# W' products by quarters of the model width on four column groups, block transposes on VectorE, and one-hot bursts kept apart

## The chip, the core and the metric

The kernel runs on one core of a Trainium2 chip. A core has TensorE (PE, matmuls into the eight banks of PSUM), VectorE (DVE), ScalarE (ACT), GpSimd (POOL) and SyncE (SP, which only issues transfers here). The metric is the time of one execution on the device in microseconds; the time of a kernel is the median of its runs.

## The reference

Tokens `x` are 2,048 rows of 640. The output mixes two branches with a gate per token, `g = sigmoid(sum(x * gate_w))`:

```
a = x @ dft_hid_re.T ;  b = x @ dft_hid_im.T
y = dft_seq_re @ a - dft_seq_im @ b              # branch A: 2048 x 2048 by 2048 x 640, twice

q = x @ w_q                                      # branch B: 32 heads of 2 x 128
s1 = q1 @ k1.T ; s2 = q2 @ k2.T                  # 16 keys in each half: 64 x 16 scores per token
top 2 of s1, top 2 of s2, top 2 of their 4 sums -> experts e of 256, weights softmax
act = gelu(x @ u[e]) ; out = sum(weight * act * v[e])

result = g * y + (1 - g) * out
```

## The kernel before

**Arithmetic.** A product in single precision is made of three matmuls on rounded parts (`mm3`, lines 137 to 141): high by high, high by low, low by high. `split` (line 132) makes the parts: ACT copies the high part, DVE or POOL subtracts it from the value. Matmuls on unrounded f32 data are also used, in one place that the change touches.

**W'.** The scores need `x @ (w_q @ k)`. So the kernel does not form q: it first multiplies `w_q` with the keys to a matrix W' of 640 x 1,024 (64 half heads by 16 keys), kept as high and low parts in `WU[0]` and `WU[1]`, with the rows (d, in five blocks of 128) on the partitions. The products have the keys as weights (`kp`, 128 x 32: two halves r of a pair side by side, one of them zero, so that two products add up in the same 32 rows of PSUM) and `w_q` as the data that streams through. As a key product has only 32 columns of weights, four of them stand side by side on the four column groups of the array, and write the rows 32j to 32j+31 of one PSUM bank.

In the kernel before, a group G takes eight half heads; column group j holds one pair of them, and the 640 columns of d are streamed in two halves of 320 (`w_part`, line 522; four loads of `wq` a group, 32 in all, through five buffers `wq`). Two calls of `w_part` make a burst. ACT copies the two banks to `wp` (line 535). The result has the keys on the partitions, and W' needs d there: `w_transposes` (line 537) turns it by TensorE, five blocks of 128x128 with the identity `identf`, into bank 7, four blocks at one place and one at the next; ACT copies the high part to WU (line 543), DVE subtracts (line 544).

**Order of the first stage.** Branch A's sums over the sequence run all the time. They are cut in pieces: `seq_piece(n)` multiplies one 128 x 512 block of a DFT matrix (loaded to `wf`, split to the ring `WS`) with x, 5 blocks of d by 3 matmuls, into banks 0 to 4; 16 pieces are a chunk, at whose end ACT copies the five banks to `ST` (line 303). A step n is a piece and what was hung behind it by `at(n, f)`; `follow(n)` emits those in the order in which they were hung. Steps 0 to 12 also load and split x (`load_x`, `split_x`), `gate_sum` sums the gate on DVE, and `gate` (line 598) at step 14 makes the sigmoid on ACT and stores the 2,048 values to `gdr` on ACT's queue. The bursts hang behind steps 4, 6, 8, 10, 12, 14, 16, 17, 18, 19, 20, 22, 23, 24, 25 and 27 with the transposes of the group before them; the stage ends with step 30 (`N0` is 31), and the scores begin. All loads are issued by SP in program order, so a load that waits for its buffer holds back the loads behind it.

**The background.** From then on the selection of the top scores and the experts run on DVE beside the matmuls of branch A. They are generators in a `Pump`: after each `mm3`, `run_bg` adds its time (0.68 us) to a clock `bg.now` and, times a share, to a credit, and takes as many steps of the generators as the credit pays for; a step yields its cost, or -1.0 where it cannot go on yet. `experts` (line 862) turns the chosen experts into one-hot rows and columns on DVE (`build`, three operations for two groups of tokens, into one of eight sets `mid`), and `use` (line 900) multiplies them on TensorE: a burst of 64 matmuls of 32 columns on the four column groups, into bank 7, which ACT copies to `cd` (line 889) and, after every second burst, stores to `gd` with two transfers (line 895). There are 16 such bursts. They are emitted with two groups of built sets behind (`behind(2)`), or all at once when the sets run out (`behind(0)`), and `bg.drain` at step NPC-18 takes whatever is left. `NPC` is 152, the number of pieces; the last quarter of branch A's sums, 16 pieces, begins at NPC-16.

Of the kernel before, what the change touches and what calls it, by code (L numbers as in the profile page):

```python
# [8 lines left out]
F32 = mybir.dt.float32  # L9
# [3 lines left out]
OP = mybir.AluOpType  # L13
# [3 lines left out]
P = 128  # L17
# [11 lines left out]
KD = D // P  # L29
HALF = D // 2  # L30
NG = HH // 8
NB = 4
GSCALE = 32768.0
FAR = -3.0e38
# [66 lines left out]
def gated_mix_kernel(ctx: ExitStack, tc: tile.TileContext, xT, xn, dreT, dimT, wsre, wsim, wq, kT, uT, vv, gw, out):  # L101
# [17 lines left out]
    def ps_s(shape=(P, TC)):  # L119
        return bank(5 + rotate("pss", 2), shape)  # L120

    def ps_t(shape, dt=F32):
        return bank(7, shape, dt)
# [94 lines left out]
    def at(n, f, *args):  # L218
        then.setdefault(n, []).append(lambda: f(*args))
# [272 lines left out]
    gate_sum(1)  # L492
    io = p1.tile([P, P], F32)
    identf = const.tile([P, P], F32)
    wtab4 = const.tile([P, E, 4], F16)
# [4 lines left out]

    def fill_ident():
        nc.gpsimd.iota(io, pattern=[[1, P]], base=0, channel_multiplier=-1, allow_small_or_imprecise_dtypes=True)
        nc.gpsimd.tensor_scalar(identf, io, 0.0, None, op0=OP.is_equal)

    def fill_rest():
        nc.gpsimd.iota(wtab4, pattern=[[-1, E], [0, 4]], base=E, channel_multiplier=0,
                       allow_small_or_imprecise_dtypes=True)

    at(1, fill_kp)
    at(4, fill_ident)  # L510
    at(6, fill_rest)

    wqs, wps, wp = {}, {}, {}
    WQB = 5
    NWQ = 4 * NG

    def load_wq(m):
        if m < NWQ:
            wqs[m] = p1.tile([P, 4, HALF], F32, name="wq", bufs=WQB)
            nc.sync.dma_start(wqs[m], wq[m])  # L520

    def w_part(m):
        G, r, n = m // 4, m // 2 % 2, m % 2
        if r == 0:
            wps[G, n] = ps_s()
        ps = wps[G, n]
        w = wqs.pop(m)
        for j in range(4):
            nc.tensor.matmul(ps[32 * j:32 * j + 32, :HALF], kp[:, 8 * G // H, r, :], w[:, j], start=(r == 0),  # L529
                             stop=(r == 1))  # L530
        load_wq(m + WQB)
        if r == 1:
            if n == 0:
                wp[G] = p1.tile([P, D], F32, name="wp", bufs=1)
            nc.scalar.activation(wp[G][:, n * HALF:(n + 1) * HALF], wps.pop((G, n))[:, :HALF], AF.Copy)  # L535

    def w_transposes(G, k0, k1):
        f = wp[G]
        t = ps_t([P, 4, P])
        for k in range(k0, k1):  # L540
            nc.tensor.transpose(t[:, k - k0, :], f[:, k * P:(k + 1) * P], identf)  # L541
        h, l = (WU[G // 4][:, n, k0:k1, P * (G % 4):P * (G % 4 + 1)] for n in range(2))
        nc.scalar.activation(h, t[:, :k1 - k0], AF.Copy)  # L543
        nc.vector.tensor_sub(l, t[:, :k1 - k0], h.bitcast(F32))  # L544

# [29 lines left out]
    for n in range(NT - 2):  # L575
        at(n, gate_sum, n + 2)
    for m in range(WQB):
        at(m, load_wq, m)

    bursts = [4 + m if m < 14 else 17 + (m - 14) * 10 // 16 for m in range(0, NWQ, 2)]  # L580
    n = bursts[-1]
    bursts += [n + 1, n + 2]
    for j, b in enumerate(bursts):
        if j >= 2:
            at(b, w_transposes, j // 2 - 1, *((4, KD) if j % 2 else (0, 4)))
        if 2 * j < NWQ:
            at(b, w_part, 2 * j)
            at(b, w_part, 2 * j + 1)
    n += 3
    at(n - 8, load_xT, 0)  # L590
# [271 lines left out]
    def experts():  # L862


        cd = {}

# [32 lines left out]

        def use(group):  # L900
            shape = (P, 16, E * 2)
            t = bank(7, shape)
            for a, (g, c, s) in enumerate(group):
                pt, qt = (HOT[s // 2][:, n, s % 2].rearrange("p (m c j) -> p m c j", m=16, j=2) for n in range(2))
                for m in range(16):
                    for j in range(2):
                        r = slice(64 * (m % 2) + 32 * j, 64 * (m % 2) + 32 * j + 32)
                        nc.tensor.matmul(t[r, 8 * a + m // 2, :], pt[:, m, :, j], qt[:, m, :, j], start=True,  # L908
                                         stop=True)
                free_sets.append(s)  # L910
            bg.now += 0.9 * len(group)
            bg.credit += 0.9 * len(group)
            whole = len(group) == 2 and group[0][1] % 2 == 0
            for a, (g, c, s) in enumerate(group[:1] if whole else group):
                sums(g, c, t if whole else t[:, 8 * a:8 * a + 8])
                yield 0.2
# [7 lines left out]
        while todo:  # L924
            if len(free_sets) < min(2, len(todo)):
                yield from behind(0)
            while todo[0][0] and len(rowed) < NT:
                yield -1.0
            k = min(len(todo), 2)
            group = [(*todo.popleft(), free_sets.popleft()) for n in range(k)]  # L930
            (g, c, s), odd = group[0], group[-1][2] % 2
            assert k == 1 or s % 2 == 0 and odd
            yield from build(g, c, s, k, 1.2 if k == 2 else 0.75)
            built.append(group)
            yield from behind(2)
# [263 lines left out]
    for n in range(N0, NPC):  # L1199
# [21 lines left out]
        if n == NPC - 28:  # L1221
            mid_wf.clear()
            for t in [t for t in wf_tags if t[0] is None]:
                wf_tags.remove(t)
        if n == NPC - 18:
            bg.drain()
# [56 lines left out]
```

## Time and profile before

| | |
|---|---|
| median of 3 runs | 766.51 us (764.39, 766.51, 767.0) |
| the profiled execution | 764.58 us, span 762.7 us |
| granted clock of TensorE | 1.00 |
| bytes moved | 162.00 MB, mean 212 GB/s |
| loads of `wq` | 32 of 640 KB, 6.9 us from issue to landing (median) |

The span is what the profile shows from the first instruction to the last; the time of the execution has about 2 us more around it. The chain of work that ended last is followed back from the last instruction; its rows give start, duration, engine and line. A row of the timeline gives start, duration, engine, line, operation, tiles, shapes and count, and in brackets how long the engine stood idle before and for what. A row of the windows gives the stretch, its length, the busy time of PE, PEld, DVE, ACT and POOL with the count of instructions, the granted clock, the share of the DMA engines and GB/s. PE rows overlap, since matmuls are pipelined: one of 512 columns is busy for 0.39 us, and the next starts 0.23 us after it.

### The profile page before, as it was taken

To read this page: it belongs to the slowest core of one execution; us is meant where nothing else is said; L and a number is where in the kernel's file an instruction comes from. 1 tells how busy PE (TensorE), PEld (TensorE's weight loads), DVE (VectorE), ACT (ScalarE), POOL (GpSimd) and SP (SyncE) were. 2 spreads that over 40 slices of the span, in tenths; PEclk is the share of its full clock that TensorE was granted. 3 is DMA by queue.
4 is the path that set the end of the run, shared out by engine and by line. 5 is a ranking of instruction groups with operands and counts; after the bars stand their busy time and mean duration, and the time that the engine had idled before them with its cause. 6 is when DMAs were issued, how large, how long until landed. Compare 5 with 4: busy or idle time off the path is not lost.

```text
span 762.7 us, 12203 instructions
## 1 busy us (share of the span) xinstructions
PE 754.8 (99%) x4568; PEld 611.1 (80%) x4568; DVE 584.7 (77%) x667; ACT 303.5 (40%) x500; POOL 371.8 (49%) x283
## 2 busy tenths in 40 slices
PE   9999999999999999999999999999899999999997
PEld 6777667888888888888888888787788888888886
DVE  7742031377989999999999999999779999648661
ACT  5334224322323452435232464444345553543441
POOL 4523224456756494757475501642013484587253
PEclk9999999999999999999999999999999999999999
DMA  9976985636455657372944868799754785776302
GB/s 337 390 263 195 292 338 218 204 120 215 138 189 159 196 195 256 106 232 94 319 149 144 267 202 254 213 359 283 206 190 141 261 301 169 226 255 196 125 28 70
DMA packets 109629, 162.00 MB, mean 212 GB/s; under 512 B 34497, under 2 KB 49985, under 8 KB 109569
## 3 DMA queue, kind: packets, MB, share of 16 engines
q1 hardware_dynamic: 78960, 133.02, 52.8%
q10 hardware_dynamic: 26960, 15.87, 7.0%
q0 software_dynamic: 3648, 12.32, 4.7%
q8 instruction: 36, 0.59, 0.3%
q14 instruction: 25, 0.20, 0.1%
HBM read 122.90 MB, written 36.71 MB: 209 GB/s over the span
## 4 chain that ended last, share of the span: by engine, by line
PE 98%; ACT 1%; DMA 0%; ACTq 0%; issue 0%; DVE 0%; DVEq 0%
PE b L139 32%; PE b L141 31%; PE b L140 31%; PE b L529 2%; PE b L908 1%; PE b L541 1%; PE b L293 0%; DMA xr<-in_xn 0%; ACT WS L134 0%; ACT ST L303 0%; ACT L599 0%; ACT cd L889 0%; ACTq L895 0%; ACT wp L535 0%; DVE ST L1173 0%
## 5 line engine op out<-in xcount | busy, mean ns | idle before, releaser
L139 PE MATMUL b<-WS,X 128*128 128x512 f32 x520 | 205.6, 395 | 0.4 <-ACT ST L303 0.3
L140 PE MATMUL b<-WS,X 128*128 128x512 f32 x520 | 202.8, 390 | 0.0
L141 PE MATMUL b<-WS,X 128*128 128x512 f32 x520 | 202.6, 390 | 0.0
L135 POOL TENSOR_TENSOR WS<-wf,WS 128x512 fp32r<-128x512 f32 x76 | 111.5, 1473 | 154.9 <-ACT WS L134 139.3
L139 PEld LDWEIGHTS b<-WS,X 128*128 128x128 f32 x520 | 97.6, 188 | 29.7 <-issue 7.8
L134 ACT ACTIVATE WS<-wf 128x512 fp32r<-128x512 f32 x116 | 72.7, 629 | 117.6 <-PE b L141 43.7
L141 PEld LDWEIGHTS b<-WS,X 128*128 128x128 f32 x520 | 97.6, 188 | 20.8
L140 PEld LDWEIGHTS b<-WS,X 128*128 128x128 f32 x520 | 97.7, 188 | 19.4 <-DVE WS L135 0.2
L635 ACT ACTIVATE sc<-b 128x512 f32<-128x512 f32 x32 | 19.5, 608 | 118.5 <-PE b L141 109.0
L135 POOL TENSOR_TENSOR WS<-ra,WS 128x512 fp32r<-128x512 f32 x40 | 59.1, 1495 | 11.8 <-ACT WS L134 11.5
L141 PE MATMUL b<-WU,xl 128*128 128x512 f32 x160 | 62.2, 389 | 0.0
L139 PE MATMUL b<-WU,xh 128*128 128x512 f32 x160 | 62.2, 389 | 0.0
L140 PE MATMUL b<-WU,xh 128*128 128x512 f32 x160 | 62.2, 389 | 0.0
L135 POOL TENSOR_TENSOR WP<-ra,WP 128x512 fp32r<-128x512 f32 x20 | 32.4, 1635 | 47.8 <-ACT WP L134 47.8
L650 DVE TENSOR_TENSOR ew<-sc,mm 128x1024 f16<-128x1024 f32 x32 | 54.4, 1700 | 1.1
L134 ACT ACTIVATE WS<-ra 128x512 fp32r<-128x512 f32 x56 | 35.1, 631 | 49.7 <-PE b L141 31.2
L1028 DVE TENSOR_TENSOR ra<-ra 128x512 f32<-128x512 f32 x48 | 49.9, 1086 | 2.9 <-POOL WP L135 2.7
L544 DVE TENSOR_TENSOR WU<-b,WU 128x512 fp32r<-128x512 f32 (+1 forms) x16 | 7.8, 490 | 57.5 <-ACT WU L543 57.5
L648 DVE TENSOR_REDUCE mm<-sc 128x64 f32<-128x1024 f32 x32 | 38.9, 1215 | 16.4 <-ACT sc L635 15.9
L314 POOL DMA_DIRECT2D tq<-td x32 | 17.6, 552 | 56.2 <-PE b L141 56.2
L654 DVE TENSOR_REDUCE rr<-ew 128x64 f16<-128x1024 f16 x32 | 39.0, 1220 | 1.1
L652 DVE TENSOR_TENSOR ew<-ew 128x1024 f16<-128x1024 f16 x32 | 37.4, 1168 | 1.1
(190 smaller groups left out, 1547.7 us busy)
## 6 DMA issues: line engine op xcount, KB each, us to landing
wq<-in_wq SPq DMA_DIRECT2D x32, 640.0 KB, 6.9
ra<-pd SPq DMA_DIRECT2D x70, 256.0 KB, 3.9
wf<-in_wsre SPq DMA_DIRECT2D x63, 256.0 KB, 4.7
wf<-in_wsim SPq DMA_DIRECT2D x46, 256.0 KB, 3.9
sa<-in_wsim SPq DMA_DIRECT2D x32, 256.0 KB, 3.0
sd<-sa SPq DMA_DIRECT2D x32, 256.0 KB, 3.2
tq<-td POOLq DMA_DIRECT2D x32, 256.0 KB, 5.1
xf<-in_xT SPq DMA_DIRECT2D x8, 640.0 KB, 5.4
```

The lines of the kernel that those rows point to most:

```text
L134: nc.scalar.activation(h, f, AF.Copy)
L135: eng.tensor_sub(l, f, h.bitcast(F32))
L139: nc.tensor.matmul(o, wh, ah, start=first, stop=False, skip_group_check=more)
L140: nc.tensor.matmul(o, wh, al, start=False, stop=False, skip_group_check=more)
L141: nc.tensor.matmul(o, wl, ah, start=False, stop=last, skip_group_check=more)
L314: nc.gpsimd.dma_start(t.bitcast(F32), td[k, :, ("s1", "s3", "a22", "s2").index(what)])
L635: nc.scalar.activation(scs[i].rearrange("p h e -> p (h e)")[:, c], ps, AF.Copy)
L648: nc.vector.tensor_reduce(m, sc, op=OP.max, axis=AX.X)
L650: nc.vector.tensor_tensor(eq, sc, m[:, :, None].to_broadcast([P, HH, E]), op=OP.is_equal)
L652: nc.vector.tensor_tensor(eq, eq, wtab, op=OP.mult)
L654: nc.vector.tensor_reduce(r, eq, op=OP.max, axis=AX.X)
L1028: nc.vector.tensor_add(take((b, o, k)) if f is not None else raw[b, o, k], raw[b, o, k] if f is None else f, raw[b, what, k])
```

## The change

1. **W' by quarters of d.** A column group no longer holds a pair of heads but a quarter of d, and a head pair's 640 columns become 160 on each group (5 blocks k of 32). Three head pairs are streamed together, 480 columns, in a burst of 8 matmuls into one bank: 11 bursts (`W_BURSTS`), ten of three pairs and one of two. The sixth crosses from the first half of the pairs to the second, which has other keys, and is made in two parts of 160 and 320 columns. They hang behind steps 6, 9, 12, 14, 16, 18, 20, 22, 24, 26 and 28.
2. **Block transposes.** As the four quarters lie on the four strips of 32 partitions, only 32x32 blocks have to be turned: `wq_out`, one step behind the burst, has one DVE transpose of 128x480 from PSUM to `wr`, from which ACT writes the high part to WU and DVE subtracts the low. The transposes on TensorE, the copies to `wp` and the identity go.
3. **Loads.** `wq` lies in memory by partition now, 163,840 bytes each, burst after burst. A burst is four loads of 480 KB (128 x 960 values; the last burst 2 x 320 each), and there are two buffers of four loads. The loads of bursts 0 and 1 hang one behind each of the steps 0 to 7; those of burst b+2 stand behind burst b, two at its step and two at the next.
4. **One-hot bursts.** `use` waits until `bg.now` is 3.0 us past the last burst; a burst adds 0.85 a group to the credit and nothing to `bg.now`; when the sets run out, one group is used and not all; the drain moves from NPC-18 to NPC-15.

```diff
+W_BURSTS = [range(n, min(n + 3, H)) for n in range(0, H, 3)]
...
-    for j in range(4):
-        nc.tensor.matmul(ps[32 * j:32 * j + 32, :HALF], kp[:, 8 * G // H, r, :], w[:, j], start=(r == 0),
-                         stop=(r == 1))
-    load_wq(m + WQB)
-    if r == 1:
-        if n == 0:
-            wp[G] = p1.tile([P, D], F32, name="wp", bufs=1)
-        nc.scalar.activation(wp[G][:, n * HALF:(n + 1) * HALF], wps.pop((G, n))[:, :HALF], AF.Copy)
...
-    for k in range(k0, k1):
-        nc.tensor.transpose(t[:, k - k0, :], f[:, k * P:(k + 1) * P], identf)
...
+    def load_wq(b, *parts):
+        if b < len(W_BURSTS):
+            c, n = W_BURSTS[b][0] * 2 * D, len(W_BURSTS[b])
+            if b not in wqs:
+                wqs[b] = p1.tile([P, 2, 4, 3 * KD * 32], F32, name="wq", bufs=2)
+            for i in parts:
+                nc.sync.dma_start(wqs[b][:, i // 2, i % 2 * 2:i % 2 * 2 + 2, :n * KD * 32],
+                                  wq[:, c:c + n * 2 * D].rearrange("p (i j x) -> p i j x", i=4, j=2)[:, i])
+
+    def w_burst(b):
...
+        for half, lo, hi in ((0, 0, k), (1, k, len(ms))):
...
+            c = slice(lo * KD * 32, hi * KD * 32)
+            for r in range(2):
+                for j in range(4):
+                    nc.tensor.matmul(ps[32 * j:32 * j + 32, c], kp[:, half, r, :], w[:, r, j, c], start=(r == 0),
+                                     stop=(r == 1))
+
+    def wq_out(b):
+        ms = W_BURSTS[b]
+        f = p1.tile([P, 3, KD, 32], F32, name="wr", bufs=1)
+        nc.vector.transpose(f[:, :len(ms)].rearrange("p i k e -> p (i k e)"), wps.pop(b)[:, :len(ms) * KD * 32])
...
+            nc.scalar.activation(h, t, AF.Copy)
+            nc.vector.tensor_sub(l, t, h.bitcast(F32))
...
+    for i in range(8):
+        at(i, load_wq, i // 4, i % 4)
+    for b, n in enumerate((6, 9, 12, 14, 16, 18, 20, 22, 24, 26, 28)):
+        at(n, w_burst, b)
+        at(n, load_wq, b + 2, 0, 1)
+        at(n + 1, wq_out, b)
+        at(n + 1, load_wq, b + 2, 2, 3)
...
         def use(group):
+            while bg.now < last[0] + 3.0:
+                yield -1.0
...
-            bg.now += 0.9 * len(group)
-            bg.credit += 0.9 * len(group)
+            last[0] = bg.now
+            bg.credit += 0.85 * len(group)
...
-                yield from behind(0)
+                yield from behind(len(built) - 1)
...
-        if n == NPC - 18:
+        if n == NPC - 15:
             bg.drain()
```

On PE, behind piece 14 (`b` is a bank of PSUM, `WS` and `X` the parts of the DFT block and of x), before:

```order
L140 MATMUL b_150<-WS,X 128x512
L141 MATMUL b_150<-WS,X 128x512
L541 MATMUL b_612<-identf,wp 128x128
L529 MATMUL b_559<-wq,kp 32x320 x4
L529 MATMUL b_566<-wq,kp 32x320 x4
L139 MATMUL b_146<-WS,X 128x512
```

and in the changed kernel, at the same place (its lines are numbered one to six lower):

```order
L139 MATMUL b_148<-WS,X 128x512
L140 MATMUL b_148<-WS,X 128x512
L528 MATMUL b_572<-wq,kp 32x480 x8
L138 MATMUL b_144<-WS,X 128x512
L139 MATMUL b_144<-WS,X 128x512
```

The transpose is gone, and eight matmuls of 320 columns into two banks are eight of 480 into one; behind pieces 4, 8, 10, 17, 19, 23, 25 and 27 no burst stands any more, and behind 9, 26 and 28 stands one that was not there.

On ACT, around the end of the first chunk (`zc` is the gate, `gdr` its store, `ST` the copies of the five banks), before:

```order
L543 ACTIVATE WU<-b_612 128x128
L535 ACTIVATE wp<-b_559 128x320
L535 ACTIVATE wp<-b_566 128x320
L599 ACT_TABLE_LOAD
L599 ACTIVATE zc<-zc 128x16
L600 DMA gdr<-zc 128x16x1
L134 ACTIVATE WS<-wf 128x512
L303 ACTIVATE ST<-b_146 128x512
```

and in the changed kernel:

```order
L542 ACTIVATE WU<-wr 128x5x96
L133 ACTIVATE WS<-wf 128x512
L593 ACT_TABLE_LOAD
L593 ACTIVATE zc<-zc 128x16
L594 DMA gdr<-zc 128x16x1
L133 ACTIVATE WS<-wf 128x512
L302 ACTIVATE ST<-b_144 128x512
```

The copies of the burst behind piece 14 stood ahead of the gate; now the write of the burst behind piece 12 does, with a split between them, and that of the burst behind piece 14 comes after the five copies to `ST`.

On ACT, at the last one-hot bursts (`cd` is the copy of bank 7, `gd` its stores, `ring` and `mid` further places of the split blocks), before:

```order
L889 ACTIVATE cd<-b_5144 128x32x16
L134 ACTIVATE WS<-wf 128x512 x2
L889 ACTIVATE cd<-b_5239 128x32x16
L895 DMA gd<-cd 1024x1x32 x2
L889 ACTIVATE cd<-b_5307 128x32x16
L889 ACTIVATE cd<-b_5374 128x32x16
L895 DMA gd<-cd 1024x1x32 x2
L134 ACTIVATE WS<-mid 128x512
```

and in the changed kernel:

```order
L883 ACTIVATE cd<-b_5136 128x32x16
L889 DMA gd<-cd 1024x1x32 x2
L133 ACTIVATE ring<-mid 128x512
L133 ACTIVATE ring<-wf 128x512
L883 ACTIVATE cd<-b_5223 128x32x16
L324 ACTIVATE ST<-b_3515 128x512
L324 ACTIVATE ST<-b_3516 128x512
L133 ACTIVATE WS<-wf 128x512
L883 ACTIVATE cd<-b_5311 128x32x16
L889 DMA gd<-cd 1024x1x32 x2
```

The last three copies stood together; splits and the copies of other banks stand between them now. On PE, 15 ordinary matmuls or more lie between any two bursts.

More of the change, by code (lines that the diff above doesn't have):

```diff
@@ L29 @@
 KD = D // P
-HALF = D // 2
-NG = HH // 8
 NB = 4
+W_BURSTS = [range(n, min(n + 3, H)) for n in range(0, H, 3)]
 GSCALE = 32768.0
@@ L492, in gated_mix_kernel @@
     gate_sum(1)
-    io = p1.tile([P, P], F32)
-    identf = const.tile([P, P], F32)
     wtab4 = const.tile([P, E, 4], F16)
@@ L499, in fill_kp @@
             nc.gpsimd.tensor_copy(kp[:, :, r, r * E:(r + 1) * E], kt)
-    def fill_ident():
-        nc.gpsimd.iota(io, pattern=[[1, P]], base=0, channel_multiplier=-1, allow_small_or_imprecise_dtypes=True)
-        nc.gpsimd.tensor_scalar(identf, io, 0.0, None, op0=OP.is_equal)
     def fill_rest():
@@ L509, in gated_mix_kernel @@
     at(1, fill_kp)
-    at(4, fill_ident)
     at(6, fill_rest)
[L513 to L527, printed above, removed]
-        for j in range(4):
-            nc.tensor.matmul(ps[32 * j:32 * j + 32, :HALF], kp[:, 8 * G // H, r, :], w[:, j], start=(r == 0),
-                             stop=(r == 1))
-        load_wq(m + WQB)
-        if r == 1:
-            if n == 0:
-                wp[G] = p1.tile([P, D], F32, name="wp", bufs=1)
-            nc.scalar.activation(wp[G][:, n * HALF:(n + 1) * HALF], wps.pop((G, n))[:, :HALF], AF.Copy)
@@ L537, in w_transposes @@
-    def w_transposes(G, k0, k1):
-        f = wp[G]
-        t = ps_t([P, 4, P])
-        for k in range(k0, k1):
[L541 to L544, printed above, removed]
+    wqs, wps = {}, {}
+    NWH = H // 2
+    def load_wq(b, *parts):
[6 more added lines that the diff above has]
+                                  wq[:, c:c + n * 2 * D].rearrange("p (i j x) -> p i j x", i=4, j=2)[:, i])
@@ new lines, in w_burst @@
+    def w_burst(b):
+        ms = W_BURSTS[b]
+        wps[b] = ps = ps_s((P, TC))
+        w = wqs.pop(b)
+        k = sum(m < NWH for m in ms)
+        for half, lo, hi in ((0, 0, k), (1, k, len(ms))):
+            if lo == hi:
+                continue
+            c = slice(lo * KD * 32, hi * KD * 32)
[3 more added lines that the diff above has]
+                                     stop=(r == 1))
@@ new lines, in wq_out @@
+    def wq_out(b):
+        ms = W_BURSTS[b]
+        f = p1.tile([P, 3, KD, 32], F32, name="wr", bufs=1)
+        nc.vector.transpose(f[:, :len(ms)].rearrange("p i k e -> p (i k e)"), wps.pop(b)[:, :len(ms) * KD * 32])
+        for i, m in enumerate(ms):
+            if i and m % NWH:
+                continue
+            n = min(len(ms) - i, NWH - m % NWH)
+            t = f[:, i:i + n].rearrange("p i k e -> p k i e")
+            h, l = (WU[m // NWH][:, a, :, 32 * (m % NWH):32 * (m % NWH + n)].rearrange("p k (i e) -> p k i e", i=n)
+                    for a in range(2))
+            nc.scalar.activation(h, t, AF.Copy)
+            nc.vector.tensor_sub(l, t, h.bitcast(F32))
@@ L576, in gated_mix_kernel @@
         at(n, gate_sum, n + 2)
[L577 to L589, printed above, removed]
+    for i in range(8):
[5 more added lines that the diff above has]
+        at(n + 1, load_wq, b + 2, 2, 3)
+    n = 30
     at(n - 8, load_xT, 0)
@@ L862, in experts @@
     def experts():
-        cd = {}
+        cd, last = {}, [0.0]
         def build(g, c, s, n, us):
@@ L1260 @@
     x = ins["A_x"][0]
+    wq = ins["B_w_q"].reshape(KD, 4, 32, H // 2, 2, 2, P).transpose(6, 5, 3, 4, 1, 0, 2).reshape(P, H, 2, 4, KD * 32)
     arrays = {
@@ L1267 @@
         "wsim": seq(ins["A_dft_seq_im"]),
-        "wq": rows(ins["B_w_q"].reshape(2, HALF, H // 8, 4, 2, 2, P).transpose(5, 2, 4, 0, 6, 3, 1)
-                   .reshape(4 * NG, P, 4, HALF)),
+        "wq": rows(np.concatenate([wq[:, b[0]:b[-1] + 1].transpose(0, 2, 3, 1, 4).reshape(P, len(b) * 2 * D)
+                                   for b in W_BURSTS], axis=1)),
         "kT": rows(np.stack([ins["B_k1"].T, ins["B_k2"].T], axis=1)),
```

## The prediction

> **What bounds the kernel now.** I read the busy table of the page first, then the chain that ended last, then the windows of the two stretches that the change touches.
>
> ```profile
> PE 754.8 (99%) x4568; PEld 611.1 (80%) x4568; DVE 584.7 (77%) x667; ACT 303.5 (40%) x500; POOL 371.8 (49%) x283
> by line: PE b L139 31.6%; PE b L141 30.7%; PE b L140 30.7%; PE b L529 2.5%; PE b L908 1.2%; PE b L541 0.6%; PE b L293 0.5%; DMA xr<-in_xn 0.4%; ACT WS L134 0.2%; ACT ST L303 0.2%; ACT L599 0.2%; ACT cd L889 0.2%; ACTq L895 0.2%; issue 0.1%;
> 20.00:138.00 118.00, 117.75 (x693) 84.36 (x692) 37.70 (x60) 41.56 (x82) 42.03 (x33) 1.00 0.80 281
> 466.00:549.00 83.00, 80.92 (x1325) 64.42 (x1324) 79.29 (x90) 36.56 (x62) 28.81 (x32) 1.00 0.87 264
> ```
>
> TensorE is busy for 99% of the span and carries nearly the whole chain. So a microsecond of matmul stream that is taken away is a microsecond of the end, as long as nothing else becomes late. The window rows give span, then PE, PEld, DVE, ACT, POOL busy time, the granted clock, the DMA share and GB/s. In the first stretch (20 to 138 us, the W' products) DVE works 37.7 of 118 us and ACT 41.6, so both have room. In the second (466 to 549 us, the one-hot bursts) DVE works 79.3 of 83 us. The clock is 1.00 in both, so no term below is scaled.
>
> **Term 1, the W' products.** Three places of the chain show what they cost today: a burst alone, one behind a single transpose, one behind four.
>
> ```profile
> 21.84 0.23 PE b L141
> 22.07 1.22 PE b L529 x16
> 23.28 0.43 PE b L139
> 23.71 0.24 PE b L140
> ...
> 47.32 0.11 PE b L541
> 47.43 1.21 PE b L529 x16
> 48.65 0.43 PE b L139
> ...
> 38.63 0.44 PE b L541 x4
> 39.08 1.21 PE b L529 x16
> 40.29 0.43 PE b L139
> ```
>
> An ordinary matmul takes 0.23 us of the chain. A burst takes 1.22, and the matmul behind it 0.43, so 0.20 more, and the next four 0.01 more each: 1.46 us. With one transpose it is 0.11 + 1.21 + 0.20 + 0.04 = 1.56, with four 0.44 + 1.21 + 0.20 + 0.03 = 1.88. The program has 16 bursts: two alone, seven of each other kind; a last group of four transposes and a last single one stand alone (0.5 and 0.1). Together 2 x 1.46 + 7 x 1.56 + 7 x 1.88 + 0.6 = 27.6 us. The shares by line agree: L529 and L541 have 3.1% of 762.7, 23.7 us, and 16 x 0.24 behind the bursts makes 27.5.
>
> The new bursts do the same number of column steps, 32 x 160 columns on four groups, in 11 pieces and not 16, and no transposes. What a wider burst costs is seen inside an old one, in narrow slices of the timeline:
>
> ```profile
> 22.00 0.48 PE L529 MATMUL b<-wq,kp 128*32 128x320 f32 x4
> 22.56 0.45 PE L529 MATMUL b<-wq,kp 128*32 128x320 f32 x4
> 22.83 0.45 PE L529 MATMUL b<-wq,kp 128*32 128x320 f32 x4
> ```
>
> Four matmuls, one on each column group, start together, and the next four start 0.27 us later (22.83 - 22.56): a burst is four such rounds of 320 columns. At 480 columns a round takes 0.27 x 1.5 = 0.405, so a burst grows by 4 x 0.135 = 0.54 to 2.00 us. Were the whole burst to scale, it would be 2.2; were the start of a round to cost something of its own, below 2.00. I take 2.00, since start and end of a burst (1.46 - 1.08 = 0.38) do not depend on its width. Nine full bursts make 18.0, the sixth, which crosses from one half of the heads to the other in eight shorter rounds, 2.05 with a little for the seam, the last, of 320 columns, 1.46. Sum 21.5 us, **saving 6.1** (4.3 if all of a burst scales).
>
> What the transposes become: 11 block transposes of 128x480 on DVE, 12 copies on ACT and 12 subtractions on DVE, for 16 + 16 copies on ACT and 16 subtractions on DVE.
>
> ```profile
> L544 DVE TENSOR_TENSOR WU<-b,WU 128x512 fp32r<-128x512 f32 (+1 forms) x16 | 7.8, 490 | 57.5 <-ACT WU L543 57.5
> L458 DVE CUSTOM_DVE_ANT_0 xr<-xr,gwb 128x640 f32<-128x640 f32 x12 | 15.8, 1312 | 0.0
> 20.56 0.82 DVE L135 TENSOR_TENSOR X<-xr,X 128x640 fp32r<-128x640 f32 x1
> 26.79 0.39 PE L139 MATMUL b<-WS,X 128*128 128x512 f32 x1
> ```
>
> No block transpose is in this trace. By the nearest rows it takes between 0.49 us (a subtraction of the same data) and 1.3 us (the slowest operation of the stretch); I take 0.7. The Vector Engine (DVE) Microarchitecture Reference of the Trainium skill (3.8, reshape front-end) says that it sustains one element per cycle and lane, which at the 0.96 GHz of the skill's main page (NeuronCore Architecture) would be about 0.5 us, an estimate; the sum would be the same. For at either end, 11 x 1.3 + 12 x 0.7 = 23 us come in for 7.8, on an engine that idles 80 us of this stretch. The transpose waits for a burst that ended a whole step (15 matmuls, 3.4 us) before; queued behind it on DVE are the low halves of x, and these are early: the one that ends at 21.38 feeds the step that starts at 26.79, and without the first burst that step starts 1.5 us sooner. WU is first read two steps after the last write. So DVE and ACT cost nothing here; without that cover, each late write would show as one wait of under 1.5 us.
>
> **Term 2, the wait at the end of step 15.**
>
> ```profile
> 65.69 0.77 ACT L535 ACTIVATE wp<-b 128x320 f32<-128x320 f32 x2 [0.83 <-PE b L529]
> 66.47 1.28 ACT L599 ACT_TABLE_LOAD   x1
> ...
> 68.01 0.39 ACTq L600 DMA_DIRECT2D gdr<-zc  x1
> ...
> 69.03 0.39 PE L141 MATMUL b<-WS,X 128*128 128x512 f32 x1
> 69.04 2.53 ACT L303 ACTIVATE ST<-b 128x512 f32<-128x512 f32 x5
> 69.67 0.50 PE L139 MATMUL b<-WS,X 128*128 128x512 f32 x1 [0.25 <-ACT ST L303]
> ```
>
> ACT waits for the burst (L535), then loads the sigmoid's table, and so comes late to copy the five full banks; PE starts its next chunk 0.64 us after the last matmul, not 0.23, and a start after a gap costs another 0.11 (0.50 for 0.39). The changed order has no copy of W' ahead of the table load: ACT is there as soon as step 13 has freed a slot, at about 4.7 + 14 x 3.4 + 3 x 2.0 = 58.5, and issues the store of the gate at about 60.8, not 68.0. **Saving 0.5** (between 0, if another wait takes the place, and 0.5).
>
> **Term 3, what that earlier store meets.** Behind it the transfers nearly stop:
>
> ```profile
> 70.00:75.00 5.00, 5.00 (x36) 3.40 (x34) 0.53 (x1) 3.20 (x7) 1.78 (x2) 1.00 0.76 151
> 75.00:80.00 5.00, 5.00 (x37) 3.34 (x33) 0.46 (x2) 0.71 (x2) 1.30 (x1) 1.00 0.60 33
> 80.00:85.00 5.00, 5.00 (x35) 3.58 (x35) 0.26 (x1) 1.55 (x3) 1.29 (x1) 1.00 0.79 248
> 85.00:100.00 15.00, 15.00 (x94) 10.65 (x88) 1.41 (x3) 4.28 (x8) 3.88 (x3) 1.00 1.02 401
> ```
>
> From about 72 to 82 us 33 to 151 GB/s move, and 401 after it. The store writes 2,048 single words; that it is the cause is inferred from its place. Before, five buffers of 640 KB lie ahead of PE, and PE has no gap there. The new program has two buffers of 1.97 MB (four loads of 480 KB), and the load of burst b+2 waits on SP for the end of burst b. With the store 7 us sooner the slow stretch falls at about 65 to 75 us. Burst 5, counted from 0, is loaded from the end of burst 3, about 4.7 + 15 x 3.4 + 4 x 2.0 = 63.7, into the middle of it. Its 1.97 MB and one piece of 0.26 then need 5.6 us at 401 GB/s, to 80.6, or a microsecond less with what trickles through (33 GB/s for 10 us). PE wants them at 4.7 + 19 x 3.4 + 5 x 2.0 = 79.3. A wait of 0.3 to 1.3 us, or none if the slow stretch is shorter: I take **0.5 lost**. On SP the loads of the pieces stand behind the waiting loads, but they go out five steps ahead of PE.
>
> **Term 4, the one-hot bursts.**
>
> ```profile
> 467.32 0.60 PE b L908 x63
> 467.92 0.43 PE b L139
> ...
> 544.23 0.66 PE b L908 x61
> 544.91 0.61 ACT cd L889
> 545.54 0.52 ACTq L895
> 546.10 0.69 ACTq L895
> 546.91 0.61 ACT cd L889
> 547.56 0.66 PE b L908 x64
> 548.22 0.43 PE b L139
> ```
>
> A burst alone costs 0.60 + 0.20 + 0.03 = 0.83 us; 13 of them, two 0.1 longer, make 11.0. The last three stand back to back, and since all use bank 7, each waits until ACT has copied the one before and issued its stores: 544.23 to 548.22 and the slow restart, 4.22 us. In the new order the closest two have 15 ordinary matmuls between them, 3.4 us; ACT needs 0.61 for the copy and 1.21 for two stores. So 16 x 0.83 = 13.3 for 15.2: **saving 1.8** (1.6 if the two long ones stay long and more follow; 0 if the waits only move). DVE builds the same one-hots, some one or two pieces later, up to a burst in the second piece of the last quarter. The bound is that DVE, busy 79.3 of 83 us, then holds up a split that PE waits for; up to the 1.8 gained.
>
> **Sum.** 6.1 + 0.5 - 0.5 + 1.8 = 7.9 us. The profiled execution took 764.58 (span 762.7 and 1.9 around it): 756.7. Its time is 1.9 below the median of the three runs, which would give 758.6. The four known executions lie in two pairs, 764.4 and 764.6, 766.5 and 767.0; I forecast from their middle, 765.5, and say **757.6 us**. A measurement of this kernel can tell about 0.3% (2.3 us) from no change, so faster means below 764.2.
>
> **Rivals.**
> - *W' comes late more than once.* From the end of burst 2 (55) to the start of the last (123.5) the new program moves 13.1 MB of W', 17 pieces of 0.26, and 2.6 of stores and small loads: 20.3 MB in 68 us, less 9 lost to the store, or 342 GB/s against the 401 seen. For: with two buffers nothing is in store, and a late burst delays the next load. Against: the margin of 15%. At 320 GB/s it costs 4 us: about 761.5.
> - *Slower: the new layout of W' loads badly.* Rows were 5,120 bytes of one block; now each partition reads 3,840 bytes from its own row of 163,840. This trace has no such pitch. If it brings the rate below 20.3 / (59.4 + 7.9) = 302 GB/s, three quarters of 401, the gain is gone; at 280 the stretch is 13 us longer, some 771 us. Against it: the whole slack of 15% goes first. A rule of the Trainium skill speaks for this rival: DMA: Bandwidth & Descriptors (Latency and other measured facts) has row pitches at large powers of two slow down, 512 KiB to 207 GB/s of 214, 4 MiB to 103. By its figures 160 KiB would lose at most 3%, an estimate, and this rival would not come; no run here shows it.
> - *The spacing only moves the waits* (DVE or ACT late at the same place): 1.8 less, 759.4. For it speaks DVE's 96%; against it that PE idles only 83.00 - 80.92 = 2.1 us in that stretch, and the chain puts them between the last three bursts, behind ACT.
> - *A burst scales as a whole* (2.2, not 2.00), so the fewer bursts save only 4.3: also 759.4. The rows of the rounds speak against it.
>
> **Chances.** Forecast (no or one short wait) 0.62; W' late by 2 to 6 us 0.18; spacing without effect 0.10; bursts that scale 0.04; slower by the layout 0.06. The range takes the low pair of executions with the full gain (6.1 + 0.5 + 1.8 = 8.4, and 0.5 should rounds grow by less than their width: 755.5, rounded to 755.0) and reaches up to 762.5, W' late by 5. Faster 0.62 + 0.10 + 0.04 + most of 0.18 = 0.91, same 0.04, slower 0.05.
>
> **What would show it.** Chain: 11 bursts of 2.0 us, no transposes, 21.5 us in all; step 15 to 16 without the 0.64. Windows: 33 GB/s some 7 us earlier, then perhaps one idle of PE ahead of the sixth burst that ends with a DMA of wq. One-hot bursts all alone at 0.6. I am wrong if PE has waits for wq at several bursts, if a round of 480 takes over 0.41, or if DVE's block transposes take over 2 us.

## The result and the profile after

| | before | changed |
|---|---|---|
| median (range) of six runs | 765.88 us (764.39 to 767.0) | 758.03 us (756.76 to 759.05) |
| ratio of the two, 95% interval | | 0.9899 (0.9881 to 0.9918) |
| profiled execution (span) | 764.58 us (762.7) | 759.05 us (757.3) |

The medians differ by 7.85 us. The two profiled executions differ by 5.5: that of before is near the fastest of its six, that of the changed kernel is the slowest of its six. What follows explains the 5.4 us between the two spans; 0.1 lies around them.

The busy table of the page, its chain by line, and the windows of the two stretches of the changed kernel (W' products 20 to 132 us, one-hot bursts 461 to 552 us):

```profile
PE 750.0 (99%) x4464; PEld 604.9 (80%) x4464; DVE 591.9 (78%) x674; ACT 296.5 (39%) x480; POOL 376.4 (50%) x281
PE b L138 30%; PE b L139 29%; PE b L140 29%; PE b L528 2%; DMA wq<-in_wq 2%; DMA mid<-in_wsim 1%; PE b L904 1%; DVE WS L134 1%; DMA mid<-sd 1%; PE b L292 1%; DMA gd<-cd 0%; PE b L480 0%; DVE mid L875 0%; ACTq L889 0%; SPq L191 0%
20.00:132.00 112.00, 111.26 (x587) 77.99 (x586) 48.38 (x67) 35.99 (x62) 40.27 (x31) 1.00 0.86 290
461.00:552.00 91.00, 89.65 (x1359) 70.32 (x1358) 82.49 (x96) 38.71 (x68) 31.13 (x31) 1.00 0.83 251
```

TensorE is still busy for 99%, at clock 1.00. What is new in the chain are transfers: `wq` with 2%, `mid` with another 2%. The chain of the kernel before has less than 1% of transfers.

**The W' bursts.** The chain at a full burst, and at the sixth:

```profile
41.30 1.75 PE b L528 x16
43.05 0.43 PE b L138
43.48 0.24 PE b L139
...
68.14 0.60 SPq L514
...
68.79 12.71 DMA wq<-in_wq
...
81.55 1.54 PE b L528 x18
83.09 0.43 PE b L138
```

A full burst is 1.75 in the chain and 0.20 in the matmul behind it. Counted over the starts of all matmuls it costs 2.00 us, nine times alike, and the last 1.47. The sixth waits: a load of `wq` that SP issued at 68.14 needs 12.71 us. The timeline of PE has the burst's first part beginning at 79.89, and the rest only at 81.55:

```profile
79.57 0.39 PE L140 MATMUL b<-WS,X 128*128 128x512 f32 x1
79.89 0.93 PE L528 MATMUL b<-wq,kp 128*32 128x160 f32 x12
81.55 1.28 PE L528 MATMUL b<-wq,kp 128*32 128x160 f32 x18 [0.74 <-DMA wq<-in_wq]
```

From 79.89 to the next ordinary matmul at 83.09 are 3.20 us; without a wait this burst takes 1.76 (first row of e3 below). So the wait costs 1.4 us with its slow restart. Why the load is so slow is in the windows of 5 us (the last number of a row is GB/s, the one ahead of it the share of the DMA engines' time):

```profile
60.00:65.00 5.00, 5.00 (x31) 2.86 (x30) 1.34 (x2) 3.01 (x5) 2.58 (x2) 1.00 0.92 257
65.00:70.00 5.00, 5.00 (x23) 4.10 (x23) 0.66 (x1) 4.12 (x7) 0.29 (x1) 1.00 0.84 29
70.00:75.00 5.00, 5.00 (x31) 2.82 (x30) 0.68 (x1) 0.00 (x0) 1.00 (x1) 1.00 0.71 81
75.00:80.00 5.00, 5.00 (x26) 3.87 (x28) 0.83 (x1) 1.13 (x2) 1.28 (x1) 1.00 1.00 380
80.00:85.00 5.00, 4.26 (x41) 2.48 (x40) 1.21 (x2) 0.63 (x1) 1.31 (x2) 1.00 1.03 408
```

The engines count as busy for 84% and 71%, and move 29 and 81 GB/s. This is the slow stretch of before, at 65 to 75 us now. Behind it the new layout of W' moves at 380 and 408 GB/s. VectorE's block transposes take 0.68 us each, and the subtractions behind them 0.87 (groups by line; busy time, mean ns):

```profile
L534 DVE STREAM_TRANSPOSE wr<-b 128x480 f32<-128x480 f32 x10 | 6.8, 680 | 16.1 <-PE b L528 16.1
L543 DVE TENSOR_TENSOR WU<-wr,WU 128x480 fp32r<-128x480 f32 x9 | 7.8, 866 | 14.4 <-ACT WU L542 14.4
```

**The one-hot bursts.** The chain at one of the last, which stood back to back before:

```profile
529.41 0.59 PE b L904 x61
530.00 0.43 PE b L138
530.43 0.23 PE b L139
```

All 16 cost 0.83 us now (one 0.91): 13.4 against 15.2, 1.8 less.

**Two new waits.** In the timeline of PE, some 15 us apart:

```profile
496.75 0.39 PE L138 MATMUL b<-WS,X 128*128 128x512 f32 x1
497.88 0.50 PE L139 MATMUL b<-WS,X 128*128 128x512 f32 x1 [0.73 <-DVE WS L134]
...
512.16 0.39 PE L140 MATMUL b<-ring,X 128*128 128x512 f32 x1
513.16 0.50 PE L138 MATMUL b<-ring,tq 128*128 128x512 f32 x1 [0.62 <-ACT ST L324]
```

The starts lie 1.12 and 1.00 us apart and not 0.23, and each restart costs 0.11: 1.9 us together. The profile of before has no such gap here. The first ends with VectorE's half of a split, the second with ACT's copy to `ST`.

**The sum of the two profiles.** W' bursts without waits 27.8 to 21.4: 6.4 less. Gap at the end of step 15 gone: 0.5 less. One-hot bursts: 1.8 less. Wait ahead of the sixth burst: 1.4 more. Two new waits: 1.9 more. 6.4 + 0.5 + 1.8 - 1.4 - 1.9 = 5.4, the difference of the spans.

### The profile page after: what moved, and what is told of

Its sections match the earlier page's. It is cut to its first block, busy times and chain, and to the rows that moved or that the text cites. A ratio compares the mean times of both kernels' runs of the same rounds, so it can differ in the third digit from the quotient of the medians.

```text
span 757.3 us, 11967 instructions
## 1 busy us (share of the span) xinstructions
PE 750.0 (99%) x4464; PEld 604.9 (80%) x4464; DVE 591.9 (78%) x674; ACT 296.5 (39%) x480; POOL 376.4 (50%) x281
## 4 chain that ended last, share of the span: by engine, by line
PE 91%; DMA 4%; DVE 2%; issue 1%; SPq 1%; ACTq 0%; ACT 0%; DVEq 0%
PE b L138 30%; PE b L139 29%; PE b L140 29%; PE b L528 2%; DMA wq<-in_wq 2%; DMA mid<-in_wsim 1%; PE b L904 1%; DVE WS L134 1%; DMA mid<-sd 1%; PE b L292 1%; DMA gd<-cd 0%; PE b L480 0%; DVE mid L875 0%; ACTq L889 0%; SPq L191 0%
## 5 line engine op out<-in xcount | busy, mean ns | idle before, releaser
L644 DVE TENSOR_TENSOR ew<-sc,mm 128x1024 f16<-128x1024 f32 x32 | 51.5, 1610 | 1.1
L646 DVE TENSOR_TENSOR ew<-ew 128x1024 f16<-128x1024 f16 x32 | 39.6, 1239 | 1.1
L134 DVE TENSOR_TENSOR WS<-wf,WS 128x512 fp32r<-128x512 f32 x40 | 33.1, 837 | 8.2 <-ACT WS L133 7.7
```

Of the source, the lines that this page charges most:

```text
L134: eng.tensor_sub(l, f, h.bitcast(F32))
L644: nc.vector.tensor_tensor(eq, sc, m[:, :, None].to_broadcast([P, HH, E]), op=OP.is_equal)
L646: nc.vector.tensor_tensor(eq, eq, wtab, op=OP.mult)
```

## The experiments

Three questions were open: whether the parts add up, what holds up the sixth burst, and where the waits near 497 and 512 us come from. The runs were made in three groups, each on one chip, and each is given as a ratio to the kernel before on that chip. A gain in us is that ratio's, unless it is said to be of the medians or the profiles.

### The change again, and its two parts alone

`e0_after_again` is the changed kernel, on the chip of the next three.

> The changed kernel once more, to see whether the two waits of PE near 497 and 512 us (1.9 us together) belong to it. Theory A (they come with the new places of the one-hot bursts and their stores): both are there again, at the same places, whatever the time. Theory B (they are a matter of the single execution; the executions of this kernel lie in two pairs, near 757 and near 759): an execution near 757 has none of them, one near 759 has both.

Measured: 759.52 us (757.91 to 760.73) against 767.05, ratio 0.9909 (0.9894 to 0.9924). Its profile (760.70) has two of the three waits, and they are larger: the sixth burst costs 3.85 us over the starts (3.36 in the changed kernel's first profile), and behind 512.54 TensorE starts nothing for 2.28. Near 497 it has no gap; a one-hot burst at 508 us costs 0.5 more instead. So theory A holds for one of the two waits only:

```profile
512.54 0.39 PE L140 MATMUL b<-ring,X 128*128 128x512 f32 x1
514.82 0.50 PE L138 MATMUL b<-ring,tq 128*128 128x512 f32 x1 [1.90 <-ACT ST L324]
```

`e1_w_only` has the W' part alone, with the old order of one-hot bursts:

```diff
-            while bg.now < last[0] + 3.0:
-                yield -1.0
...
-            last[0] = bg.now
-            bg.credit += 0.85 * len(group)
+            bg.now += 0.9 * len(group)
+            bg.credit += 0.9 * len(group)
...
-                yield from behind(len(built) - 1)
+                yield from behind(0)
...
-        if n == NPC - 15:
+        if n == NPC - 18:
```

> The W' part alone, one-hot bursts as before. By the traces: bursts and transposes 27.8 us before and 22.8 after with the wait ahead of the sixth burst in it, so 5.0 less, and 0.5 less at the end of step 15: 5.5 us less than before, about 760.4. The last three one-hot bursts stand together and cost 4.2 us as before. If theory A holds, no waits near 497 and 512 us; if B, they may be there or not.

Measured: 760.76 us, ratio 0.9935 (0.9913 to 0.9956): 5.0 less (3.4 to 6.7), 6.3 by the medians. The W' bursts and the late sixth (3.13 us) are those of the changed kernel. There are no gaps near 497 and 512. The last three one-hot bursts stand back to back again and cost 6.3 us with what follows, not the 4.2 expected: TensorE waits 0.5 us longer between them, and behind them the matmuls run at half speed (see the last section).

`e2_onehot_only` has the one-hot part alone, the reverse of this diff on the kernel before.

> The one-hot part alone on the kernel before. 16 bursts at 0.83 us for 15.2 in all: 1.8 us less than before, about 764.1. If theory A holds, the two waits come with it and take 1.9 back: no difference, 765.9.

Measured: 764.99 us, ratio 0.9985 (0.9973 to 0.9998): 1.2 less (0.2 to 2.1), 2.1 by the medians. Its one-hot bursts cost 13.4 us, and it has no gap near 497 and 512 either. Its profiled time (764.48) is no lower than that of before all the same, since a load of `wq` is late by 0.7 us at 84 us, and the slow matmuls at the start of every execution last to 6.2 us and not to 3.7.

The ratios multiplied give 0.9920, the whole change has 0.9909: the parts add up within the intervals. But only kernels with both parts show a wait at 497 or 512.

### The gate's store

`e3_gate_rows` is the changed kernel with the gate turned by one 32x32 block transpose on VectorE, and stored as 64 runs of 128 bytes, by POOL, in place of 2,048 single words:

```diff
-        nc.scalar.activation(zc, zc, AF.Sigmoid)
-        nc.scalar.dma_start(gdr.rearrange("(i p) -> p i", p=P), zc)
+        nc.scalar.activation(zc[:, :NT], zc[:, :NT], AF.Sigmoid)
+        nc.vector.transpose(zt, zc)
+        for b in range(4):
+            nc.gpsimd.dma_start(gdr.rearrange("(i b p) -> b i p", b=4, p=32)[b], zt[32 * b:32 * b + NT])
```

> The changed kernel with the gate's 2,048 values turned by one DVE block transpose and stored as 64 runs of 128 bytes by four transfers on POOL's queue, in place of 2,048 single words. Theory (the single words hold up all transfers for some 10 us, and that makes the sixth W' burst late): no stretch under 150 GB/s between 60 and 80 us, no wait ahead of the sixth burst, which then takes 2.05 us for 3.36: 1.3 us less than the changed kernel, about 756.7. Rival (two buffers are too few whatever the store does): the wait stays, 758.

Measured: 757.02 us (756.62 to 757.53), ratio 0.9875 (0.9861 to 0.9890), 2.5 less than the changed kernel beside it. The sixth burst in its chain, and its windows:

```profile
80.11 1.76 PE b L530 x32
```

```profile
65.00:70.00 5.00, 5.00 (x24) 4.10 (x22) 0.66 (x1) 4.00 (x7) 2.05 (x3) 1.00 0.95 320
70.00:75.00 5.00, 5.00 (x31) 2.83 (x30) 1.22 (x2) 1.24 (x2) 2.17 (x2) 1.00 0.62 209
```

320 and 209 GB/s where 29 and 81 were, and no wait, with the same two buffers. So the store of single words is the cause, and two buffers are enough without it. (The edit also moves the store from ACT's queue to POOL's, and no run tells the two apart; but the issue on ACT took only 0.39 us, and what came late was a load that SP had issued.) A gain of 1.3 us was expected and 2.5 measured: in the profiles the sixth burst costs 1.98 for 3.85, and the gap near 512 is 0.74 for 2.28. The second of these also differs between executions of one kernel (below).

`e6_gate_before` makes the same edit in the kernel before.

> The kernel before with only the gate's store changed as in e3 (32x32 block transpose on DVE, 64 runs of 128 bytes). Theory: the kernel before had the slow stretch too (33 to 151 GB/s for 10 us) but five buffers covered it, so its removal brings at most the few tenths that one late burst cost: 0 to -0.7 us, a ratio of 0.999 to 1.000. Rival: the store costs any kernel about what it cost the changed one (2.5 us): a ratio near 0.997.

Measured: 765.34 us against 766.76, ratio 0.9985 (0.9975 to 0.9994): 1.2 us less (0.5 to 1.9), where 0 to 0.7 were expected and 2.5 by the rival. Its slow stretch is gone (140 and 314 GB/s from 70 to 80 us), and so is the gap of 0.64 us at the end of step 15, though the sigmoid's table is loaded at the same place of ACT's order; only the store's issue no longer stands between it and the copies to `ST`. Behind the first 25 us, that gap of 0.5 us is all in which the two profiles differ, and in neither does TensorE wait for `wq`: five buffers hid the slow stretch, and the cost of the store that these profiles show is its place on ACT's queue. The rest of the 1.2 us is not explained; the interval reaches down to 0.5.

### Fewer bursts, or no transposes

`e4_two_pairs_rows` is e3 with bursts of two pairs: 16 bursts of 320 columns as in the kernel before, but without transposes on TensorE.

```diff
-W_BURSTS = [range(n, min(n + 3, H)) for n in range(0, H, 3)]
+W_BURSTS = [range(n, min(n + 2, H)) for n in range(0, H, 2)]
...
-                wqs[b] = p1.tile([P, 2, 4, 3 * KD * 32], F32, name="wq", bufs=2)
+                wqs[b] = p1.tile([P, 2, 4, 2 * KD * 32], F32, name="wq", bufs=3)
```

> The kernel e3_gate_rows (757.0 us) with bursts of two pairs in place of three: 16 bursts of 320 columns, still no transposes on TensorE, three buffers of W' loads in place of two. It splits the W' gain into 'no transposes' and 'fewer bursts'. Theory of the prediction: a burst has a fixed part of about 0.38 us beside the rounds, so 16 bursts of 320 columns cost 16 x 1.47 = 23.5 us, 2.0 more than e3's 21.5: about 759.0, a ratio to the kernel before near 0.990. Rival: a burst costs in proportion to its columns and the whole W' gain comes from the transposes that go: 757.0, as e3.

Measured: 759.31 us (759.09 to 759.63), ratio 0.9907 (0.9891 to 0.9924). In its chain:

```profile
39.24 1.21 PE b L530 x16
40.45 0.43 PE b L138
```

Every burst costs 1.47 us over the starts, 16 make 23.5, and e3's eleven make 21.5. The profiled times differ by 2.2 us (759.16 and 756.96), the ratios by 2.4. A burst's fixed part is as the prediction had it: of the 6.4 us some 4.4 come from the transposes, 2.0 from the fewer bursts.

### The waits near 497 and 512 us

Here the DMA engines and VectorE are both full (the windows below). Only the first profile of the changed kernel has the wait at 497 us; the other, at ACT's copy to `ST`, comes back in e0, e3, e4 and e10. The chain of the changed kernel there names who was late:

```profile
503.14 8.64 DMA mid<-in_wsim
...
511.80 0.67 ACTq L889
...
512.51 0.60 ACT ST L324
...
513.16 0.50 PE b L138
```

A load of `mid` takes 8.64 us, then ACT issues a store of `gd`, then makes the copy that TensorE needs. The first guess took the store on ACT's queue for the cause. `e5_gd_on_sp` has SP issue it:

```diff
-                    nc.scalar.dma_start(gd[g, n, :, :, :, :, w].rearrange("s j e f m -> (s j e) f m"),
+                    nc.sync.dma_start(gd[g, n, :, :, :, :, w].rearrange("s j e f m -> (s j e) f m"),
```

> The kernel e3_gate_rows (757.0 us) with the stores of the one-hot products (gd) issued by SP in place of ACT. Theory: the waits of TensorE near 497 and 512 us, which only kernels with both parts of the change have shown, arise because ACT's queue stands behind the issue of these stores while the DMA engines are full, with the copies and splits that PE needs behind them. Then they go: no PE gap over 0.3 us between 490 and 520 us, 0.7 to 1 us less, about 756.2. Rival 1: the loads of that stretch are late themselves: the waits stay and the time is 757.0. Rival 2: SP, which issues all loads in order, is now held back by the wait for ACT's copy: loads of pieces late, slower by 1 us or more.

Measured: 757.47 us (756.26 to 758.79), ratio 0.9882 (0.9865 to 0.9900), no better than e3. The waits in the timeline of its PE near 510 us:

```profile
507.81 0.66 PE L908 MATMUL b<-mid 128*32 128x32 f16 x64 [0.58 <-ACT cd L887]
510.93 0.50 PE L139 MATMUL b<-WS,X 128*128 128x512 f32 x1 [0.64 <-DVE WS L134]
```

The wait for the copy to `ST` is gone, and two others stand in its place, together longer. They go back to loads: ACT stands idle for 5.32 us ahead of a split at 504 us, until a load of `wf` lands. SP had issued this load and its four neighbours late: by the count of ordinary products that TensorE had begun, between the 2131st and the 2157th, and in the kernel before between the 2106th and the 2132nd. So e5 does not clear the store on ACT's queue. It took one wait away and brought others, as the second rival had it (SP held back), though the trace does not show that the stores held SP back. `e7_before_again`, the kernel before profiled once more, asked whether they come and go by chance:

> The kernel before once more, for a second profile. If the waits of PE near 497 and 512 us come and go with the execution whatever the kernel, they may show here too (0.5 to 2 us). If they belong to the two parts of the change together, there are none, and a time in the upper half (767) differs from the lower one (764.6) elsewhere, for instance in how long the matmuls at the start run at half speed (3.3 to 6.2 us so far).

764.80 us, and no gap near 497 or 512. To see where the lateness begins, count how many ordinary products TensorE had begun when VectorE finished one and the same subtraction of a split, the one that ends at 500.5 us in the kernel before:

| before | e7 | e6 | e2 | e1 | changed | e0 | e3 | e4 | e10 | e9 | e8 |
|---|---|---|---|---|---|---|---|---|---|---|---|
| 2132 | 2132 | 2128 | 2131 | 2129 | 2142 | 2141 | 2142 | 2141 | 2142 | 2129 | 2127 |

(e8 to e10 follow below; e5 is 2132 here and falls behind a few splits later.) Where the waits appear, VectorE is 9 or 10 products later than in the kernel before, a little over 2 us, and SP, which waits for the buffer that the subtraction frees, issues its next load as much later. (The place is chosen where the difference is large: at the next seven splits the changed kernel is at most 6 products later.) That suggested VectorE as the cause. But VectorE had also waited itself, at 472 us in the changed kernel, for a split's copy that ACT made behind the issue of two stores of `gd`:

```profile
468.93 2.67 ACTq L889 DMA_DIRECT2D gd<-cd  x2
471.64 1.15 ACT L133 ACTIVATE WS<-wf 128x512 fp32r<-128x512 f32 x2 [2.75 <-issue]
472.31 2.12 DVE L134 TENSOR_TENSOR WS<-wf,WS 128x512 fp32r<-128x512 f32 x1 [2.17 <-ACT WS L133]
```

At this place VectorE waits for 0.8 to 2.2 us in all six kernels that have both parts and issue both stores on ACT, and for 1.0 in e2. It waits for 0.2 in before, e7, e6 and e1, and not at all in e5, whose stores SP issues, and in e9, which has half of them. `e8_dve_later` is e3 with 4 us of one-hot work moved behind the crowded stretch:

```diff
+        bg.credit += {100: -4.0, 118: 4.0}.get(n, 0.0)
```

> The kernel e3_gate_rows (757.0 us) with VectorE's one-hot operations kept out of the crowded stretch: from step 100 to step 118 of the 152 the background has 4 us less of credit, given back after it. Theory: the waits near 497 and 512 us come from VectorE, which is full there: its subtractions end 8 to 11 products later than in the kernel before, SP's loads wait for the buffers that they free, and the loads then come in a bunch (6.6 to 7.2 us from issue to landing, 5.5 to 6.3 without the waits). Then the gap of 0.74 us near 510 goes, the latency falls to 6.3 or less, and the time is 0.5 to 1 us below e3: about 756.3. Rival: the transfers themselves are too many there, whatever VectorE does: the gap stays, 757.0, or the postponed one-hots collect at the end and cost up to 1 us more: 758.0.

`e9_half_gd` takes work from the DMA engines in place of VectorE: half of the stores of `gd` are left out, so half of the experts' one-hot products are missing in its output.

> The kernel e3_gate_rows (757.0 us) with half of the stores of the one-hot products left out (the second of the two gd stores of each group; that half of gd is filled once at step 40 with values of no meaning, so the experts' rows are not the reference's). VectorE's work is unchanged; the crowded stretch has 2 or 3 stores of 1,024 runs of 128 bytes less. Theory (VectorE late): the waits near 510 us stay, 0.5 to 1.5 us, and the time stays at 757.0. Rival (the transfers are too many there): the gap goes and the latency of the loads at 490 to 505 us falls below 6 us: about 756.3.

`e10_gate_rows_again` is e3 on the same chip.

> The kernel e3_gate_rows once more, on the chip of the two runs beside it, to compare with them and to see whether its gap near 510 us (0.74 us) comes back. Both theories expect a gap of 0.5 to 1.5 us between 490 and 520 us, since every kernel with both parts of the change has shown one; if there is none, the waits are a matter of the execution. Time 757.0, 2.0 to 2.5 below the changed kernel.

| | median (range) | ratio to before, 95% interval | gap of PE between 490 and 520 us |
|---|---|---|---|
| e8, later one-hots | 755.86 (755.74 to 756.81) | 0.9871 (0.9858 to 0.9885) | none |
| e9, half of the stores | 756.52 (756.44 to 757.11) | 0.9879 (0.9865 to 0.9892) | none |
| e10, e3 again | 757.18 (756.58 to 759.36) | 0.9896 (0.9879 to 0.9913) | 0.45 |

The stretch from 495 to 510 us, in the changed kernel, in e8 and in e9 (a window of each):

```profile
495.00:510.00 15.00, 14.27 (x184) 11.11 (x183) 15.00 (x18) 6.14 (x10) 6.48 (x10) 1.00 0.97 346
```

```profile
495.00:510.00 15.00, 15.00 (x249) 11.87 (x248) 11.25 (x14) 7.80 (x14) 2.66 (x5) 1.00 1.05 377
```

```profile
495.00:510.00 15.00, 15.00 (x188) 12.05 (x187) 14.89 (x17) 6.03 (x11) 4.58 (x8) 1.00 0.99 367
```

In e8 VectorE is busy for 11.25 us of 15 and not for all 15, and TensorE has no gap. But e9 loses the gap as well, with VectorE busy for 14.89. The loads' time from issue to landing fell in neither, though e8's theory and e9's rival expected it to (a mean of about 7.1 us over the forty products behind the 2120th in e8, 8.2 in e9, 6.0 in e10). So e9 does not show that the DMA engines are the cause: it also takes work from ACT's queue (one issue of 0.52 us ahead of the copies to `ST`, where e3 has two in 1.24), and by the table its VectorE is early at the split (2129).

What the runs show is that a gap comes with a late VectorE at that split (in e5 a few splits behind it), and that either edit takes both the gap and the lateness away. Load, split, freed buffer and next load form a loop, and ACT's issues of stores stand in it too. Which of them starts the lateness is not shown. Why each part alone stays clear of the waits is not settled either: e2 has VectorE's wait at the earlier place, and is not late at the split. e8's interval overlaps e10's, so its 1.3 us by the medians are likely, not certain. The gap also differs between two executions of one kernel (0.74 in e3 and 0.45 in e10; 1.00 in the changed kernel and 2.28 in e0), and executions without a profile can't be told apart.

e8 is the fastest kernel of the study by its ratio: 0.9871 against 0.9899 and 0.9909 for the change itself. e3, e5 and e9 lie within its interval.

## Why the prediction was right, by its own steps

It said 757.6 us, and 758.03 was measured; 7.9 us less, and 7.85 was measured between the medians.

- **Term 1** (saving 6.1): 6.4. A full burst was said to take 2.00 us and takes 2.00; the seam of the sixth was put at 2.05 and costs nothing (1.98 without its wait). That the start and end of a burst do not depend on its width was the step it rested on, and e4 shows it: 1.47 at 320 columns, 2.00 at 480.
- **The transposes on VectorE**: taken as 0.7 us, measured 0.68. By the Trainium skill's Vector Engine (DVE) Microarchitecture Reference (3.8) it would have been about 0.5, an estimate; the trace shows 0.68, and the difference does not move the sum.
- **Term 2** (saving 0.5): 0.5. The reason was half of the truth: in e6 the copy of W' and the table load stand where they stood, and the gap goes with the store's issue alone.
- **Term 3** (losing 0.5, between 0.3 and 1.3): the mechanism was right, in its place (slow from 65 to 75 us), its victim (the sixth burst) and its cause (e3). The size was too small: 1.4 us, and by the same count 1.9 in e0. The step that was off is the 2.23 MB at 401 GB/s from 75 us on, to 80.6: by the windows 1.90 MB passed to 80 us, at 380, and 0.61 more to 81.5, when the load landed; about one piece more than was counted. The restart was not counted either.
- **Term 4** (saving 1.8): 1.8 at the bursts themselves. Its bound, that VectorE then holds up a split that TensorE waits for, came true at 497 us; at 512 the wait was for ACT's copy to `ST`, which the prediction did not name. The two took 1.9 in the profiled execution, all that the spacing gained. The prediction priced this ("up to the 1.8 gained") and counted it at nothing. The runs show that it takes both parts together; what starts it is open.
- **The sum.** On the two profiles it is 5.4 us and not 7.9: terms 3 and 4 were 0.9 and 1.9 too good, term 1 was 0.3 too cautious. The medians nevertheless differ by 7.85, and by 7.5 on the chip of e0. The profiled execution of the changed kernel was its slowest, so part of the agreement to half a microsecond is luck of the executions compared. Another part has a likely reason that the prediction did not have: about half of the executions of the kernel before lose time to a lower clock, which its profile does not show and the spaced bursts seem to spare (last section). Two small sums of the prediction are off without effect (58.5 should be 58.3, and 20.3 MB about 20.1).
- **Rivals.** W' was late once, not more often. The layout is not slow: 380 and 408 GB/s, against the 302 below which the gain would have gone, and 401 in the old layout. The rule in DMA: Bandwidth & Descriptors of the Trainium skill (Latency and other measured facts), by which this pitch would lose at most 3%, an estimate, agrees. Bursts do not scale as a whole. The rival that spacing only moves the waits fell in e2, whose bursts cost 1.8 less without a new wait near them, and came true in part where both changes are together.

## What to carry to other kernels

A transfer of many single words is paid by whoever loads at that moment: before moving one, look up in the windows which transfers it will meet, and if the words can be turned into runs of 128 bytes, do that first. Where two resources are both full in a stretch, a change that takes slack out of it should be priced with a wait there, even if each part alone shows none; here a little work moved behind the stretch (e8) likely won it back. And a burst's cost splits into a fixed and a proportional part that one narrow slice of the timeline shows; that split carried the largest term here.

## What the runs showed of the hardware that was not expected

**One small store slows every other transfer.** 2,048 words of 4 bytes, 8 KB, hold the core's transfers at 29 and 81 GB/s for 10 us, while its DMA engines count as 84% and 71% busy; a 480 KB load of `wq` issued in that time took 12.71 us, where the median is 7.0 (the page's list of transfers: count, size, us to landing):

```profile
wq<-in_wq SPq DMA_DIRECT2D x40, 480.0 KB, 7.0
```

As 64 runs of 128 bytes the same 8 KB leave 320 and 209 GB/s. The words are not what fills the engines all this time: in the trace of the changed kernel all packets of 4 bytes on the store's queue start before 66 us, and it is the loads' packets of 3,840 bytes that are slow behind them, with a mean of 1.4 us each from 66 to 73 us, where large packets take 0.13 from 76 us on. Why is not shown. The Trainium skill, in DMA: Bandwidth & Descriptors (Why small descriptors are slow), gives fixed costs for each small piece; that loads on another queue are slow for 7 us after the pieces is what this trace adds.

**Half speed behind three bursts.** In the chain of e1 the matmuls behind the last three one-hot bursts take 0.43 us, not 0.23:

```profile
543.66 0.43 PE b L140
544.09 0.43 PE b L138
544.52 0.43 PE b L139
...
546.65 0.31 PE b L138
546.97 0.23 PE b L139
```

The window from 540 to 550 us, and TensorE's wait between the bursts (us, times, longest):

```profile
540.00:550.00 10.00, 8.14 (x137) 6.61 (x121) 1.39 (x2) 2.95 (x5) 0.00 (x0) 0.83 0.44 85
...
PE b L902 <- ACT cd L883: 2.6, 2, 1.9
```

The same of the kernel before:

```profile
540.00:550.00 10.00, 7.92 (x218) 6.48 (x219) 7.04 (x9) 3.66 (x6) 0.27 (x1) 1.00 0.63 161
...
PE b L908 <- ACT cd L889: 2.1, 2, 1.3
```

In e1 the granted clock is 0.83 there, and TensorE had waited 2.6 us in two pieces. In the kernel before the waits are 2.1 us, and the clock stays at 1.00. The Trainium skill (TensorE: Matmul & The Clock Gate, Part 1) has the clock halved after an idle window of about 3.4 us that runs freely; here 2.6 us of waits, with bursts of 0.66 between them, were enough once.

The record suggests that it is not rare. The mean granted clock is on record for 56 executions of kernels with the three bursts together (before, e1, e6, e7) and for 49 of kernels with all bursts apart. It is 0.997 or lower in 29 of the 56, and in one of the 49. The half speed in e1's profile lasts 3.4 us, and brings that execution to 0.998. In e6, the five executions at 0.997 take 765.7 to 766.1 us and the five at 0.999 take 764.5 to 765.0. So keeping the bursts apart likely also saves about 1 us in half of the executions. No execution at 0.997 was profiled, so the place of its slow matmuls is not shown.
